# Loading block 0's x in quarters of 256 rows by half the columns, interleaved with the w1 chunks

## The chip, the cores and the metric

The kernel runs on one core of a Trainium2 chip. The metric is the device time of one execution in microseconds (us); where several executions were timed, their median is given. Times inside the kernel come from a hardware profile and are counted from the first instruction of its span.

## The reference

The reference is a feed-forward layer with a squared ReLU, in bfloat16:

```python
B, S, D, F = 1, 2048, 576, 4608
h = jnp.einsum("bsd,df->bsf", x, w1) + b1
r = jnp.where(h > zero, h, zero)
h = r * r
out = jnp.einsum("bsf,fd->bsd", h, w2) + b2
```

There are 2048 rows of x, 576 columns each (four groups of 128 and a remainder of 64), and 4608 hidden columns, which are 36 groups of 128.

## The kernel before

The 2048 rows are handled in four blocks of 512. The first product gives hT, the hidden values with the hidden columns on the partitions, so it needs x transposed. Blocks 1 to 3 get it by transposing transfers. Block 0 is loaded as it lies and transposed on TensorE, because that is sooner to start with. For the first six groups of hidden columns (the tile `qn`, "quads" of 128 rows of w1 by 768 columns), block 0 accumulates over full 128-row contractions in six PSUM banks `bk0`. All later groups use contractions of 64 rows, two at a time in the two halves of the array.

The loads that the opening needs, and where they are issued:

```python
def load_x(eng, j):                 # one tile of 128 rows by 576 columns, 144 KB
    eng.dma_start(out=xs[:, j, :], in_=x_view[:, j, :])

def load_quad(eng, c):              # 128 rows of w1 by 768 columns, 192 KB
    eng.dma_start(out=qn[:, c, :], in_=w1[c * P:(c + 1) * P, 0:G * P])

for j in range(RT):                 # RT = 4
    load_x(nc.sync, j)
    load_quad(nc.scalar, j)
nc.scalar.activation(out=warm[:], ..., func=ACT.Relu)
for h in range(2):
    load_rest(nc.sync, h)           # the last 64 rows of w1 for the same hidden columns
for j0, n in ((3, 1), (4, 1), ..., (14, 4)):
    for h in range(2):
        load_w1(nc.sync, h, j0, n, slice(0, NH))   # w1h, for the groups after these
```

A function that runs when the program is finished moves these first loads ahead of the barrier with which the program opens. Before, the first load of each of the two queues went ahead of the queue's drain instruction, the others ahead of its wait on the barrier:

```python
for k, i in enumerate(mine[:n]):
    wanted = mybir.InstDrain if k == 0 else mybir.InstEventSemaphore
```

While the loads are on their way, TensorE runs five matmuls of 128x512 on a constant, to bring up its clock. Then come the transposes (with the identity, built on GpSimd), the copies of their results from PSUM to `xT[0]`, and the matmuls on them:

```python
def transpose_tile(j, c, n, eng):   # n column groups of row tile j; eng copies them out of PSUM
    tp = psum.tile([P, n, P], BF16, name="tp", tag="bank")
    for k in range(n):
        d0 = (c + k) * P if c < NC else D - P
        nc.tensor.transpose(tp[:, k, :], xs[:, j, d0:d0 + P], ident[:])    # L178
    c0 = c if c < NC else 7
    copy_psum(eng, xT[0][:, c0:c0 + n, cols], tp[:])                        # L169 ScalarE, L171 VectorE
    if c == NC:
        copy_psum(eng, xT[0][0:H, 8, cols], tp[H:P, 0, :])

def full_mm(j, n, c):               # row tiles j to j+n-1, column group c of x
    cols = slice(j * P, (j + n) * P)
    for q in range(G):              # G = 6
        nc.tensor.matmul(bk0[q][:, cols], lhsT=qn[:, c, q * P:(q + 1) * P], rhs=xT[0][:, c, cols],
                         start=(j == 0 and c == 0), stop=False, ...)        # L228
```

After these the bias is transposed (L254), the last 64 rows are added (L259), the six banks go through ScalarE (ReLU with bias, L192) and VectorE (square, L194), and the steps on the remaining groups follow:

```python
for i in range(GP):
    for h in range(2):
        nc.tensor.matmul(bk0[GP * h + i][:], lhsT=qr[rows, i * P:(i + 1) * P],
                         rhs=xT[0][rows, place(h, 8), :], start=False, stop=True, ...)   # L259
...
for j in range(GP, NJ):
    a_step(0, j)                    # 18 matmuls of 64x512 each, L208
```

Blocks 1 to 3 run the same steps (L208). Then the second product follows: 64 of its columns at L321, the rest at L335.

Of the kernel before, what the change touches and what calls it, by code (L numbers as in the profile page):

```python
# [11 lines left out]
BF16 = mybir.dt.bfloat16  # L12
# [5 lines left out]
def kernel(  # L18
# [9 lines left out]
    nc = tc.nc  # L28
    P = 128
    H = 64  # L30
    x2 = x.flatten_outer_dims()
    out2 = out.flatten_outer_dims()
    S, D = x2.shape
    F = w1.shape[1]
    FH = F // 2
    G = 6
# [3 lines left out]
    NC = D // P  # L40
# [4 lines left out]
    RT = SB // P  # L45
    HALF = SB // 2
# [9 lines left out]
    psum = ctx.enter_context(tc.tile_pool(name="psum", bufs=8, space=PSUM))  # L56

    def bank(name):
        return psum.tile([P, SB], FP32, name=name, tag="bank")
# [10 lines left out]
    def early(n):  # L70
        at[0] += n
        assert at[0] <= NFT * D
        return w2_sb[:, at[0] - n:at[0]]


    xT = [early(XW).rearrange("p (w s) -> p w s", s=SB) for b in range(NSB - 1)]
    xT3 = xpool.tile([P, NH, SB], BF16, name="xT3", tag="xT3")
    xT.append(xT3[:])
    xs = early(RT * D).rearrange("p (j c) -> p j c", c=D)
# [6 lines left out]
    x_view = x2.rearrange("(rt p) d -> p rt d", p=P)  # L86
# [2 lines left out]
    def w2(ft, a, b):  # L89
        return w2_sb[:, ft * D + a:ft * D + b]  # L90

    def load_x(eng, j):
        eng.dma_start(out=xs[:, j, :], in_=x_view[:, j, :])

    def load_quad(eng, c):
        eng.dma_start(out=qn[:, c, :], in_=w1[c * P:(c + 1) * P, 0:G * P])  # L96

    def load_w1(eng, h, j0, n, cs):
        f0 = pairs[j0][h] * P
        eng.dma_start(out=w1h[h * H:(h + 1) * H, cs, j0 * P:(j0 + n) * P], in_=w1_rows[:, cs, f0:f0 + n * P])  # L100
# [5 lines left out]

    b1T = const.tile([P, NFT], FP32, name="b1T")
    warm = const.tile([P, 1], FP32, name="warm")
    for j in range(RT):
        load_x(nc.sync, j)  # L110
        load_quad(nc.scalar, j)
    nc.scalar.activation(out=warm[:], in_=nc.const_aps.tensor(1.0, [P, 1], FP32), func=ACT.Relu)
    for h in range(2):
        load_rest(nc.sync, h)
# [2 lines left out]
    for j0, n in ((3, 1), (4, 1), (5, 1), (6, 1), (7, 1), (8, 1), (9, 1), (10, 2), (12, 2), (14, 4)):  # L117
        for h in range(2):
            load_w1(nc.sync, h, j0, n, slice(0, NH))


    def issue_at_barrier(nc):
        entry, body = nc.main_func.blocks[:2]
        for engine in (mybir.EngineType.SP, mybir.EngineType.Activation):
            mine = [i for i in body.instructions if i.engine == engine and not isinstance(i, mybir.InstNoOp)]
            n = 0
            while isinstance(mine[n], mybir.InstDMACopy) and not mine[n].has_wait():
                n += 1
            assert n >= RT
            for k, i in enumerate(mine[:n]):  # L130
                wanted = mybir.InstDrain if k == 0 else mybir.InstEventSemaphore
                at = next(k for k, i in enumerate(entry.instructions) if i.engine == engine and isinstance(i, wanted))
                body.instructions.remove(i)
                entry.instructions.insert(at, i)

    nc.at_finalize(issue_at_barrier)


# [17 lines left out]
    ident = const.tile([P, P], BF16, name="ident")  # L156
# [10 lines left out]
    def copy_psum(eng, dst, src):  # L167
        if eng is nc.scalar:
            nc.scalar.copy(out=dst, in_=src)  # L169
        else:  # L170
            nc.vector.tensor_copy(out=dst, in_=src)  # L171

    def transpose_tile(j, c, n, eng):
        cols = slice(j * P, (j + 1) * P)
        tp = psum.tile([P, n, P], BF16, name="tp", tag="bank")
        for k in range(n):
            d0 = (c + k) * P if c < NC else D - P
            nc.tensor.transpose(tp[:, k, :], xs[:, j, d0:d0 + P], ident[:])  # L178
        c0 = c if c < NC else 7
        copy_psum(eng, xT[0][:, c0:c0 + n, cols], tp[:])  # L180
        if c == NC:
            copy_psum(eng, xT[0][0:H, 8, cols], tp[H:P, 0, :])

    def hT_of(b, ft):
        if b < NSB - 1:
# [30 lines left out]


    V, A = nc.vector, nc.scalar
    transpose_tile(0, 0, 1, V)
    transpose_tile(0, 3, 1, V)  # L220
    transpose_tile(0, 1, 2, A)
    transpose_tile(0, NC, 1, V)
    bk0 = [bank("ph") for _ in range(G)]

    def full_mm(j, n, c):
        cols = slice(j * P, (j + n) * P)
        for q in range(G):
            nc.tensor.matmul(bk0[q][:, cols], lhsT=qn[:, c, q * P:(q + 1) * P], rhs=xT[0][:, c, cols],  # L228
                             start=(j == 0 and c == 0), stop=False, skip_group_check=True)

    full_mm(0, 1, 0)
    transpose_tile(1, 0, 2, V)
    transpose_tile(1, 2, 2, A)
    full_mm(0, 1, 1)
    full_mm(1, 1, 0)
    transpose_tile(2, 0, 2, V)
    full_mm(1, 1, 1)
    transpose_tile(2, 2, 2, A)
    full_mm(0, 2, 2)
    transpose_tile(3, 0, 2, V)  # L240
    full_mm(2, 1, 0)
    full_mm(2, 1, 1)
    transpose_tile(3, 2, 2, A)
    full_mm(2, 1, 2)
    transpose_tile(1, NC, 1, V)
    full_mm(0, 2, 3)
    transpose_tile(2, NC, 1, V)
    full_mm(3, 1, 0)
    full_mm(3, 1, 1)
    transpose_tile(3, NC, 1, A)  # L250
    full_mm(3, 1, 2)
    full_mm(2, 2, 3)
    b1T_ps = psum.tile([P, P], BF16, name="b1T_ps", tag="bank")
    nc.tensor.transpose(b1T_ps[:], b1_rows[:], ident[:])  # L254
    nc.vector.tensor_copy(out=b1T[:], in_=b1T_ps[:, 0:NFT])
    for i in range(GP):
        for h in range(2):
            rows = slice(h * H, (h + 1) * H)
            nc.tensor.matmul(bk0[GP * h + i][:], lhsT=qr[rows, i * P:(i + 1) * P], rhs=xT[0][rows, place(h, 8), :],  # L259
                             start=False, stop=True, skip_group_check=True)  # L260
# [56 lines left out]
    for pr in range(NSB // 2):  # L317
        pc = bank("pc")
        for ft in range(NFT):
            for h in range(2):  # L320
                nc.tensor.matmul(pc[h * H:(h + 1) * H, :], lhsT=w2(ft, DM, D), rhs=hT_of(2 * pr + h, ft),  # L321
                                 start=(ft == 0), stop=(ft == NFT - 1))
# [52 lines left out]
```

## Time and profile before

| What | Value |
|---|---|
| Time, median of 3 runs | 290.41 us (289.91 to 290.61) |
| Span of the profiled execution | 288.3 us, granted TensorE clock 1.000 |
| TensorE (PE) busy | 284.7 us, 99% |
| ScalarE (ACT) busy | 95.4 us, 33% |
| VectorE (DVE) busy | 79.8 us, 28% |
| x loads, issue to landing, shortest / median / longest | 2.2 / 3.7 / 4.8 us |
| w1 quads, issue to landing, shortest / median / longest | 2.6 / 4.1 / 5.2 us |

PE is TensorE's matmul row and PEld its weight loads, which run beside the matmuls. A busy matmul row includes the time in which a matmul runs through the array, so the pace of a group is better read from the starts of one group and the next. "L228" is line 228 of the kernel before. The name `w_sb` stands for the whole of one large tile in which the loaded x, the quads and the transposed x of block 0 all lie until w2 takes it; a wait for `w_sb<-in_x_dram` is a wait for an x load, one for `w_sb<-in_w_dram` a wait for a w1 load. `ph` are the PSUM banks of the first product, `tp` those of the transposes.

### The profile page before, as it was taken

What the parts mean: (1) busy time and instruction counts of PE and PEld (TensorE: products, weight loads), DVE (VectorE), ACT (ScalarE), POOL (GpSimd) and SP (SyncE); (2) the same over time, 40 slices, a digit from 0 to 9 for tenths busy, and PEclk for the clock granted to TensorE, in tenths of its full rate; (3) what the DMA queues carried; (4) which work ended last, traced back from release to release, by engine and by line L of the source; (5) the groups of instructions that cost most, each with busy time, mean ns of one, the idle gap of its engine ahead of it and who ended that gap; (6) DMA issues with size and microseconds to landing.
All of it is one profiled execution on the core that took longest, in us unless ns stands there. A gap on an engine that the chain in (4) does not pass through costs nothing.

```text
span 288.3 us, 4894 instructions
## 1 busy us (share of the span) xinstructions
PE 284.7 (99%) x2108; PEld 134.4 (47%) x2108; DVE 79.8 (28%) x200; ACT 95.4 (33%) x154; POOL 1.5 (1%) x8
## 2 busy tenths in 40 slices
PE   8999999999999999999999999999999999999996
PEld 5644444444444444444445444444444444444454
DVE  2654444544444444444420011111100011111111
ACT  3676766666676666666620000000000000000000
POOL 2000000000000000000000000000000000000000
PEclk9999999999999999999999999999999999999999
DMA  8999999910400005300000100000000000000000
GB/s 240 190 207 201 180 178 208 314 61 0 125 0 2 1 2 150 98 0 2 0 3 18 20 20 20 23 20 8 12 23 20 20 20 23 20 20 22 23 20 20
DMA packets 35381, 18.31 MB, mean 64 GB/s; under 512 B 22804, under 2 KB 35360, under 8 KB 35360
## 3 DMA queue, kind: packets, MB, share of 16 engines
q1 hardware_dynamic: 34752, 17.21, 26.7%
q10 hardware_dynamic: 576, 0.79, 0.9%
q8 instruction: 16, 0.26, 0.4%
q14 instruction: 5, 0.04, 0.1%
q0 software_dynamic: 32, 0.01, 0.0%
HBM read 12.23 MB, written 2.36 MB: 51 GB/s over the span
## 4 chain that ended last, share of the span: by engine, by line
PE 97%; DMA 2%; ACTq 0%; issue 0%; DVE 0%
PE ph L208 46%; PE po L335 43%; PE pc L321 5%; DMA w_sb<-in_w_dram 2%; PE ph L228 1%; PE ph L259 0%; ACTq L96 0%; PE tp L178 0%; DVE o_sb L337 0%; ACTq L359 0%; PE b1T_ps L254 0%
## 5 line engine op out<-in xcount | busy, mean ns | idle before, releaser
L192 ACT ACTIVATE r<-ph,b1T 128x512 bf16<-128x512 f32 x144 | 90.6, 685 | 46.0 <-PE ph L208 45.1
L208 PE MATMUL ph<-w_sb,w1h 64*128 64x512 bf16 x918 | 99.2, 376 | 0.0
L208 PEld LDWEIGHTS <-w1h 64*128 64x128 bf16 x1242 | 60.4, 94 | 73.6
L335 PE MATMUL po<-w_sb,hT 128*128 128x512 bf16 x432 | 93.4, 379 | 0.0
L335 PEld LDWEIGHTS <-hT 128*128 128x128 bf16 x432 | 42.2, 98 | 51.2 <-issue 0.4
L194 DVE TENSOR_TENSOR hT<-r 128x512 bf16<-128x512 bf16 x108 | 45.7, 425 | 52.3 <-ACT r L192 52.2
L337 DVE TENSOR_TENSOR o_sb<-po,b_bc 128x512 bf16<-128x512 f32 (+2 forms) x17 | 11.2, 660 | 116.7 <-PE po L335 116.7
L208 PE MATMUL ph<-xT,w1h 64*128 64x512 bf16 x324 | 35.1, 376 | 0.0
L335 PE MATMUL po<-w_sb,w1h 128*128 128x512 bf16 (+2 forms) x180 | 31.3, 336 | 0.0
L335 PEld LDWEIGHTS <-w1h 128*128 128x128 bf16 x180 | 16.2, 98 | 15.3
L194 DVE TENSOR_TENSOR w1h<-r 128x512 bf16<-128x512 bf16 x36 | 15.3, 425 | 19.7 <-ACT r L192 19.5
L321 PE MATMUL pc<-hT,w_sb 128*64 128x512 bf16 x108 | 15.7, 379 | 0.0
L321 PEld LDWEIGHTS <-w_sb 128*64 128x64 bf16 x144 | 8.1, 110 | 7.6 <-issue 0.4
L321 PE MATMUL pc<-w1h,w_sb 128*64 128x512 bf16 x36 | 7.9, 379 | 0.0
L228 PE MATMUL ph<-w_sb 128*128 128x128 bf16 (+1 forms) x78 | 6.5, 232 | 0.0
L323 ACT ACTIVATE oc<-pc,b2T 128x512 bf16<-128x512 f32 x2 | 1.4, 687 | 13.7 <-PE pc L321 13.7
L228 PEld LDWEIGHTS <-w_sb 128*128 128x128 bf16 x78 | 5.3, 99 | 0.5 <-DMA w_sb<-in_w_dram 0.2
L331 DVE COPY o_sb<-oc 128x64 bf16<-128x64 bf16 x16 | 2.7, 172 | 9.2 <-DMA oc<-oc 9.2
L171 DVE COPY w_sb<-tp 128x128 bf16<-128x128 bf16 (+2 forms) x11 | 2.6, 243 | 6.4 <-PE tp L178 6.3
L169 ACT COPY w_sb<-tp 128x256 bf16<-128x256 bf16 (+2 forms) x6 | 2.0, 333 | 4.5 <-PE tp L178 4.5
L178 PE MATMUL tp<-ident,w_sb 128*128 128x128 bf16 x20 | 2.9, 243 | 0.4 <-DMA w_sb<-in_x_dram 0.4
L165 PE MATMUL wps<-one 128*128 128x512 bf16 x5 | 2.3, 626 | 0.4 <-DVE one L140 0.4
(26 smaller groups left out, 10.4 us busy)
## 6 DMA issues: line engine op xcount, KB each, us to landing
w_sb<-in_w_dram SPq DMA_DIRECT2D x2, 1728.0 KB, 8.4
out_dram<-o_sb SPq DMA_DIRECT2D x15, 144.0 KB, 1.8
w1h<-in_w_dram SPq DMA_DIRECT2D x14, 144.0 KB, 4.6
w_sb<-in_w_dram SPq DMA_DIRECT2D x2, 864.0 KB, 6.9
w1h<-in_w_dram SPq DMA_DIRECT2D x4, 288.0 KB, 6.4
w1h<-in_w_dram SPq DMA_DIRECT2D x2, 576.0 KB, 10.4
w1h<-in_w_dram SPq DMA_DIRECT2D x2, 432.0 KB, 6.7
w_sb<-in_w_dram ACTq DMA_DIRECT2D x4, 192.0 KB, 4.1
```

What stands on the lines that cost most here:

```text
L165: nc.tensor.matmul(wps[:], lhsT=ones[:, 0:P], rhs=ones[:], start=(i == 0), stop=(i == NWARM - 1))
L169: nc.scalar.copy(out=dst, in_=src)
L171: nc.vector.tensor_copy(out=dst, in_=src)
L178: nc.tensor.transpose(tp[:, k, :], xs[:, j, d0:d0 + P], ident[:])
L192: nc.scalar.activation(out=r[:], in_=bk[:], func=ACT.Relu, bias=b1T[:, ft:ft + 1], scale=1.0)
L194: nc.vector.tensor_tensor(out=hT_of(b, ft), in0=r3, in1=r3, op=ALU.mult)
L208: nc.tensor.matmul(bk[h][:], lhsT=w1h[rows, c, j * P:(j + 1) * P], rhs=xT[b][rows, place(h, c), :], start=(i == 0), stop=(i == NH - 1))
L228: nc.tensor.matmul(bk0[q][:, cols], lhsT=qn[:, c, q * P:(q + 1) * P], rhs=xT[0][:, c, cols], start=(j == 0 and c == 0), stop=False, skip_g ...
L321: nc.tensor.matmul(pc[h * H:(h + 1) * H, :], lhsT=w2(ft, DM, D), rhs=hT_of(2 * pr + h, ft), start=(ft == 0), stop=(ft == NFT - 1))
L331: nc.vector.tensor_copy(out=o_sb[:, DM:D], in_=o_tr[pr][:, jj, h * H:(h + 1) * H])
L335: nc.tensor.matmul(po[:, 0:e - a], lhsT=hT_of(b, ft)[:, jj, :], rhs=w2(ft, a, e), start=(ft == 0), stop=(ft == NFT - 1))
L337: nc.vector.tensor_tensor(out=o_sb[:, a:e], in0=po[:, 0:e - a], in1=b2_bc[:, a:e], op=ALU.add)
```

## The change

x of block 0 came in four row tiles of 128 rows by all 576 columns. It now comes in four quarters: the first or second 256 rows, by the first 256 or the last 320 columns. "xa01" are the left columns of row tiles 0 and 1, "xb23" the right ones of row tiles 2 and 3. The order of issue, over both queues, is xa01, q0, q1, xa23, xb01, q2, xb23, q3. The idea is that 256 rows of two column groups, with two chunks of w1, give TensorE more to do per byte than one row tile with all its columns. The transposes are regrouped accordingly: a chunk is one column group of 256 rows (two transposes into one bank, one copy), and all the full matmuls have 256 columns. Two loads of each queue, not one, now go ahead of the drain.

```diff
-    def load_x(eng, j):
-        eng.dma_start(out=xs[:, j, :], in_=x_view[:, j, :])
+    def load_x(eng, half, a, e):
+        js = slice(2 * half, 2 * half + 2)
+        eng.dma_start(out=xs[:, js, a:e], in_=x_view[:, js, a:e])
...
-    for j in range(RT):
-        load_x(nc.sync, j)
-        load_quad(nc.scalar, j)
+    CA = 2 * P
+    load_x(nc.sync, 0, 0, CA)
+    load_quad(nc.scalar, 0)
+    load_quad(nc.sync, 1)
+    load_x(nc.scalar, 1, 0, CA)
+    load_x(nc.sync, 0, CA, D)
+    load_quad(nc.scalar, 2)
+    load_x(nc.sync, 1, CA, D)
+    load_quad(nc.scalar, 3)
...
-                wanted = mybir.InstDrain if k == 0 else mybir.InstEventSemaphore
+                wanted = mybir.InstDrain if k < 2 else mybir.InstEventSemaphore
...
-    def transpose_tile(j, c, n, eng):
...
+    def transpose_chunk(half, c, eng):
+        cols = slice(half * HALF, (half + 1) * HALF)
+        d0 = c * P if c < NC else D - P
+        tp = psum.tile([P, HALF], BF16, name="tp", tag="bank")
+        for i in range(2):
+            nc.tensor.transpose(tp[:, i * P:(i + 1) * P], xs[:, 2 * half + i, d0:d0 + P], ident[:])
+        copy_psum(eng, xT[0][:, c if c < NC else 7, cols], tp[:])
         if c == NC:
-            copy_psum(eng, xT[0][0:H, 8, cols], tp[H:P, 0, :])
+            copy_psum(eng, xT[0][0:H, 8, cols], tp[H:P, :])
...
-    transpose_tile(0, 0, 1, V)
-    transpose_tile(0, 3, 1, V)
-    transpose_tile(0, 1, 2, A)
-    transpose_tile(0, NC, 1, V)
+    transpose_chunk(0, 0, V)
+    transpose_chunk(0, 1, V)
...
-    full_mm(0, 1, 0)
-    transpose_tile(1, 0, 2, V)
-    transpose_tile(1, 2, 2, A)
-    full_mm(0, 1, 1)
-    full_mm(1, 1, 0)
-    transpose_tile(2, 0, 2, V)
-    full_mm(1, 1, 1)
-    transpose_tile(2, 2, 2, A)
-    full_mm(0, 2, 2)
-    transpose_tile(3, 0, 2, V)
-    full_mm(2, 1, 0)
-    full_mm(2, 1, 1)
-    transpose_tile(3, 2, 2, A)
-    full_mm(2, 1, 2)
-    transpose_tile(1, NC, 1, V)
-    full_mm(0, 2, 3)
-    transpose_tile(2, NC, 1, V)
-    full_mm(3, 1, 0)
-    full_mm(3, 1, 1)
-    transpose_tile(3, NC, 1, A)
-    full_mm(3, 1, 2)
-    full_mm(2, 2, 3)
+    full_mm(0, 0)                      # full_mm(half, c, qs): 256 rows, column group c
+    full_mm(0, 1, range(2))
+    transpose_chunk(1, 0, V)
+    full_mm(0, 1, range(2, G))
+    transpose_chunk(1, 1, A)
+    full_mm(1, 0)
+    transpose_chunk(0, 2, V)
+    full_mm(1, 1)
+    transpose_chunk(0, 3, A)
+    full_mm(0, 2)
+    transpose_chunk(1, 2, V)
+    transpose_chunk(0, NC, A)
+    full_mm(0, 3)
+    transpose_chunk(1, 3, V)
+    full_mm(1, 2)
+    transpose_chunk(1, NC, A)
+    full_mm(1, 3)
```

The comment on the first new `full_mm` is added here; the rest of the diff only fits the helpers to the new arguments.

More of the change, by code (lines that the diff above doesn't have):

```diff
@@ L171, in copy_psum @@
             nc.vector.tensor_copy(out=dst, in_=src)
-    def transpose_tile(j, c, n, eng):
[L174 to L180, printed above, removed]
+    def transpose_chunk(half, c, eng):
[5 more added lines that the diff above has]
+        copy_psum(eng, xT[0][:, c if c < NC else 7, cols], tp[:])
         if c == NC:
-            copy_psum(eng, xT[0][0:H, 8, cols], tp[H:P, 0, :])
+            copy_psum(eng, xT[0][0:H, 8, cols], tp[H:P, :])
     def hT_of(b, ft):
@@ L218, with full_mm @@
     V, A = nc.vector, nc.scalar
-    transpose_tile(0, 0, 1, V)
-    transpose_tile(0, 3, 1, V)
-    transpose_tile(0, 1, 2, A)
-    transpose_tile(0, NC, 1, V)
+    transpose_chunk(0, 0, V)
+    transpose_chunk(0, 1, V)
     bk0 = [bank("ph") for _ in range(G)]
-    def full_mm(j, n, c):
-        cols = slice(j * P, (j + n) * P)
-        for q in range(G):
+    def full_mm(half, c, qs=range(G)):
+        cols = slice(half * HALF, (half + 1) * HALF)
+        for q in qs:
             nc.tensor.matmul(bk0[q][:, cols], lhsT=qn[:, c, q * P:(q + 1) * P], rhs=xT[0][:, c, cols],
-                             start=(j == 0 and c == 0), stop=False, skip_group_check=True)
-    full_mm(0, 1, 0)
-    transpose_tile(1, 0, 2, V)
-    transpose_tile(1, 2, 2, A)
-    full_mm(0, 1, 1)
-    full_mm(1, 1, 0)
-    transpose_tile(2, 0, 2, V)
-    full_mm(1, 1, 1)
-    transpose_tile(2, 2, 2, A)
-    full_mm(0, 2, 2)
-    transpose_tile(3, 0, 2, V)
-    full_mm(2, 1, 0)
-    full_mm(2, 1, 1)
-    transpose_tile(3, 2, 2, A)
-    full_mm(2, 1, 2)
-    transpose_tile(1, NC, 1, V)
-    full_mm(0, 2, 3)
-    transpose_tile(2, NC, 1, V)
-    full_mm(3, 1, 0)
-    full_mm(3, 1, 1)
-    transpose_tile(3, NC, 1, A)
-    full_mm(3, 1, 2)
-    full_mm(2, 2, 3)
+                             start=(half == 0 and c == 0), stop=False, skip_group_check=True)
+    full_mm(0, 0)
[15 more added lines that the diff above has]
+    full_mm(1, 3)
     b1T_ps = psum.tile([P, P], BF16, name="b1T_ps", tag="bank")
```

## The prediction

> **What bounds the kernel now.** I read the page's first part, then the chain that ended last, then who waited for whom in the opening microseconds, then the timeline of that stretch.
>
> ```profile
> PE 284.7 (99%) x2108; PEld 134.4 (47%) x2108; DVE 79.8 (28%) x200; ACT 95.4 (33%) x154; POOL 1.5 (1%) x8
> ```
>
> TensorE is busy for 99% of the span. The chain (start, length, what) says where the other 1% is:
>
> ```profile
> 1.13 4.82 DMA w_sb<-in_w_dram
> 5.95 0.05 issue
> 6.00 0.83 PE ph L228 x6
> ...
> 10.54 0.06 PE b1T_ps L254
> 10.59 0.76 PE ph L259 x6
> 11.35 134.03 PE ph L208 x1242
> 145.38 15.66 PE pc L321 x144
> 161.04 124.53 PE po L335 x612
> ```
>
> From 11.35 us on the chain is TensorE without a break: 134.03 + 15.66 + 124.53 us. The change touches none of it. Before 6.00 the chain is a transfer: the third w1 chunk, issued at 1.13 and landed at 5.95. So only the opening, up to the first L208 matmul, can move, and it moves the end one for one as long as the stream behind it stays unbroken. What it has to give is its idle time. The waits of PEld (the weight loads, which hold back their matmuls) in the first 30 us give it by cause, in total, times, longest:
>
> ```profile
> PEld L178 <- DMA w_sb<-in_x_dram: 1.2, 3, 0.6
> PEld L228 <- DMA w_sb<-in_w_dram: 0.2, 1, 0.2
> ```
>
> The timeline (start, length, engine, line; in brackets the idle time before) places them:
>
> ```profile
> 2.48 0.74 PE L178 MATMUL tp<-ident,w_sb 128*128 128x128 bf16 x5
> ...
> 3.11 0.51 PE L228 MATMUL ph<-w_sb 128*128 128x128 bf16 x6
> ...
> 4.04 0.23 PEld L178 LDWEIGHTS <-w_sb 128*128 128x128 bf16 x4 [0.60 <-DMA w_sb<-in_x_dram]
> ...
> 5.21 0.11 PEld L178 LDWEIGHTS <-w_sb 128*128 128x128 bf16 x2 [0.18 <-DMA w_sb<-in_x_dram]
> ...
> 5.99 0.55 PEld L228 LDWEIGHTS <-w_sb 128*128 128x128 bf16 x6 [0.22 <-DMA w_sb<-in_w_dram]
> 6.00 0.83 PE L228 MATMUL ph<-w_sb 128*128 128x256 bf16 x6
> 6.56 0.21 PEld L178 LDWEIGHTS <-w_sb 128*128 128x128 bf16 x2
> 6.66 0.28 PE L178 MATMUL tp<-ident,w_sb 128*128 128x128 bf16 x2
> 6.72 0.71 PEld L228 LDWEIGHTS <-w_sb 128*128 128x128 bf16 x12
> 6.78 0.83 PE L228 MATMUL ph<-w_sb 128*128 128x128 bf16 x12
> ```
>
> Here is what TensorE lacks: after six matmuls on the first x tile it has nothing until the second tile lands (4.0), then again at 5.2 and 6.0. After 6.0 the data is ahead of TensorE. The starts also give each form's true pace: six matmuls of 256 columns from 6.00 to 6.66, so 0.109 us each; two transposes from 6.66 to 6.78 and twelve matmuls of 128 columns from 6.78 to 7.45, so 0.056 us each.
>
> The stage from the first L228 (3.11) to the first L208 (11.18 by the timeline) lasts 8.07 us. Its work is 60 matmuls of 128 columns (3.36 us), 18 of 256 (1.96), 15 transposes (0.84), the bias transpose, 0.16 to the next start, and six L259 matmuls, from 10.53 to 11.18 (0.65): 6.97 us. So 1.1 us is idle. That is the whole prize, 0.4% of 290.41.
>
> **What the Trainium skill says.** "TensorE: Matmul & The Clock Gate", section "Back-to-back issue gap", gives columns / 2.4 + 2.5 ns once the clock is up, 56 and 109 ns for 128 and 256 columns; the trace has just that. The same page, "What's actually happening", says that the array runs at half rate until it has been busy for some 3.4 us, in a window that does not start with the kernel. Here the five warming matmuls take 0.43 us each (0.38 to 2.48, ending at the first transpose), the first five transposes 0.63 us together, and the full pace is there from 3.11, after 2.7 us. "DMA: Bandwidth & Descriptors", "Issuing engines are not separate DMA queues", says that transfers issued by SyncE and ScalarE share 16 engines and interleave. The trace agrees: all engines' mean DMA share is 1.02 from 2 to 4 us, with both queues loading. Its "Specifications" want 512 B or more in one piece for full rate; the w1 chunks behind, in pieces of 256 B, run at some 200 GB/s with the engines full (8 to 12 us), x and w1 quads at 309 (2 to 4 us). The new quarters have pieces of 512 and 640 B, on the right side of this.
>
> **The change, part by part.**
> *Bytes per unit of work.* Before, TensorE had after 336 KB (one x tile 144, one w1 quad 192) six matmuls of 128 columns, 0.34 us of work; after 672 KB another 18 of these. Now 128 + 192 KB give six matmuls of 256 columns (0.65 us), and 192 KB more, q1, another six. At 640 KB, with xa23, there are 24 such matmuls, 2.6 us, on the table. The load total stays 1344 KB; the order is better fitted to the arithmetic.
>
> *TensorE work removed.* 60 + 18 matmuls become 48 of 256 columns: 5.23 us in place of 5.32, so 0.09 saved. Twenty transposes stay twenty; now four of them come before the first L228 and sixteen after (0.90 in place of 0.84). Work from the first L228 on: 5.23 + 0.90 + 0.16 + 0.65 = 6.94 us.
>
> *First matmul.* The warming ends at 2.48, so x landing at 2.2 is not what holds the first transposes, and a slightly slower first quarter is hidden. In the timeline VectorE's first copy begins at 2.83, 0.35 after its single transpose. Now there are two, 0.11 apart at the slow clock, and the copy is 128x256, 0.29 us (the L171 group of that shape), not 0.23. That gives 2.48 + 0.11 + 0.35 + 0.29 = 3.23 and a hand-over of 0.05: 3.3. Before it was 3.11. So the start loses 0.2.
>
> *Transfers against need.* Running on from 3.3, six matmuls of step (0,0) end at 3.95, two of (0,1) at 4.17. Then xa23 is needed; two transposes, four matmuls, two transposes and (1,0) run to 5.5. Then xb01 is needed; after (1,1) at 6.3 q2 is needed, after (0,2) at 7.0 xb23, at 7.2 q3. For the arrivals I take the bytes by time from the windows of the trace: 254 KB moved by 2.0, 872 by 4.0, 1147 by 5.0. The last byte of the old set, at 1376 thousand bytes, was moved at about 5.7 and landed at 1.61 + 5.2 = 6.8 (last w1 issue and its longest landing), a lag of up to 1.1; the first pair lagged some 0.5. With 0.8 as the middle: xa23 (655 thousand bytes) moved at 3.3, there at 4.1; xb01 and q2 (1016) moved at 4.5, there at 5.3; all at 6.5 to 6.8. Against the needs 4.17, 5.5, 6.3, 7.0, 7.2 every one is just in time, the first two with hardly a margin. I count 0.15 us for waits left at xa23 and xb01 and for a late q0, which now shares the engines with q1, issued sooner.
>
> *Barrier.* Two transfers per queue now go ahead of each queue's drain. One issue takes about 0.4 us, so the barrier, released near 0.8 before, comes near 1.2 and the identity, ready at 1.49, near 1.9. The first transpose is at 2.48: hidden.
>
> *Copies.* VectorE and ScalarE have 292 and 367 ns copies of 256 columns with 0.6 us of matmuls between; only the last remainder is tight: transposed from 8.8, with ScalarE's copies from 9.03 for 0.37 + 0.26 us (the L169 groups), it is ready at 9.7, and L259 is due at 9.6. I count 0.1.
>
> *Sum.* 3.3 + 6.94 = 10.24 with no wait, against 11.18: 0.94 gained at best. Less 0.15 and 0.1 gives 0.7.
>
> **Behind the stage.** L208 starts some 0.7 earlier and wants its w1h chunks earlier. The chunks land 3.9 to 11.2 us after issue; by the semaphore times the tightest early one, column group 5, is there at 12.8 and used at 15.1. A start 1.0 earlier still leaves 1.3. ScalarE's six squared-ReLU evictions in a row shift with it, as each needs only L259 and the bias.
>
> **The rivals.** *The wait moves* (25%): q0 and q1 share the engines, q0 lands at 3.5, and xa23 comes at 4.5. For it: some packets take long, and landings spread by over 1 us in one transfer. It would eat 0.6 to 1.0: 289.9 to 290.4. *The transfer is hidden anyway* (5%): w1h or ScalarE give the gain back at 11 to 20 us; the idle time of TensorE there is now nil and the margin 2.3 us, so I doubt it: 290.3. *Slower* (7%): more and smaller pieces with strides take longer to issue and move, so that q3 ends after 7.8, or the full clock comes later: 290.4 to 290.9. *All the idle time goes* (15%), as when the full clock comes sooner: 289.4 or below.
>
> **Range and chances.** 290.41 − 0.7 = 289.7. The three runs of before lie within 0.7 us, so a median is good to some 0.3. With the gain between 0.1 and 1.2 in eight of ten cases, the range is 289.0 to 290.4. Two per cent is 5.8 us, over five times the idle time there is; the three chances follow.
>
> **What would show it.** The first L228 at 3.1 to 3.4; TensorE's idle time on DMA before 7 us at 0.3 in total, not 1.1; all L228 at 128x256, 48 of them; the first L208 near 10.5; L208, L321 and L335 of the same lengths as now. It is wrong if PEld waits 0.5 or more for q0 or xa23, if the identity or the remainder copies release a TensorE instruction, or if L208 shows a wait that it had not.

## The result, and the profile after

The changed kernel takes 291.81 us (median of 6 runs, 291.34 to 292.58), the kernel before, run beside it on the same chip, 290.02 us (289.71 to 290.61). The ratio is 1.0061, with a 95% interval of 1.0043 to 1.0080: the change makes the kernel slower by 1.8 us, where a gain of 0.7 was predicted.

The profiled execution of the changed kernel is the slowest of the six, 292.58 us against 290.04 for that of before, so the differences read below sum to 2.5 us, not to 1.8. In the changed file L186 is the transposes, L233 the 256-column matmuls, L215 the steps that were L208; L259, L321 and L335 are what they were.

The chain that ended last (start, length, what):

```profile
0.00 3.48 DMA w_sb<-in_x_dram
3.48 0.04 issue
3.52 0.41 PE tp L186 x2
3.94 0.02 issue
3.96 0.30 DVE w_sb L179
4.26 0.04 issue
4.30 1.86 PE ph L233 x8
...
8.94 0.77 PE ph L233 x6
9.71 0.11 PE tp L186 x2
9.82 0.66 PE ph L233 x6
...
12.65 0.38 ACT w_sb L177
13.03 0.04 issue
13.07 0.82 PE ph L259 x6
13.90 134.03 PE ph L215 x1242
147.93 15.66 PE pc L321 x144
163.59 124.53 PE po L335 x612
```

The three long pieces at the end are the same to the hundredth, 134.03, 15.66 and 124.53 us; they only start later. All of the loss is ahead of 13.90. Two things stand out there. The chain begins with the very first transfer, xa01, landed at 3.48 us; its counterpart x0 landed at 2.2. And the pace: six L233 matmuls take 0.66 us at 9.82, but eight take 1.86 at 4.30.

The waits of PEld in the first 30 us (in total, times, longest) show the same from the other side:

```profile
PEld L186 <- DMA w_sb<-in_x_dram: 1.7, 1, 1.7
...
PEld L259 <- DMA w1h<-in_w_dram: 0.2, 1, 0.2
```

There is one wait for a load, and it is for the first. The later waits, for x tiles and for the third w1 chunk, which the change was made to remove, are gone. The page names a w1h load for the last line; ScalarE's copies of the remainder are what ended at 13.03, as the chain's step before L259 says.

The timeline (start, length, engine, line; idle before in brackets) shows the hole between the warming and the first transposes:

```profile
0.38 2.31 PE L173 MATMUL wps<-one 128*128 128x512 bf16 x5 [0.38 <-DVE one L148]
...
1.69 0.29 POOL masks.py:199 TENSOR_SCALAR_AFFINE_SELECT ident<-ident 128x128 bf16<-128x128 bf16 x1
...
3.52 0.61 PE L186 MATMUL tp<-ident,w_sb 128*128 128x128 bf16 x4 [0.84 <-DMA w_sb<-in_x_dram]
...
4.30 1.86 PE L233 MATMUL ph<-w_sb 128*128 128x256 bf16 x8 [0.17 <-DVE w_sb L179]
...
13.72 2.55 PE L215 MATMUL ph<-w_sb,w1h 64*128 64x512 bf16 x22
```

The identity is ready at 1.98, so it holds nothing back. L233 starts at 4.30, not 3.11 (+1.19 us), and from there to the first L215 it is 9.42 us, not 8.07 (+1.35): together the 2.54 us. For the second part one asks for the duration of single L233 matmuls (shortest/median/longest in ns, then first and last start), once for the stretch from 4.3 to 8.9 us and once from 9.2 to 13:

```profile
L233 PE MATMUL ph<-w_sb x19: 372/417/417, 4.3 to 8.7; 128*128 128x256 bf16 x19
```

```profile
L233 PE MATMUL ph<-w_sb x29: 272/273/321, 9.0 to 12.6; 128*128 128x256 bf16 x29
```

A duration includes the run through the array; from start to start it is 0.213 us before and 0.109 after about 9.0. Until then TensorE ran at half rate. Nineteen matmuls of this form and six transposes at half pace cost 19 × 0.104 + 6 × 0.05 = 2.3 us more than at full pace. With the 6.94 us of work that the prediction counted and 0.2 us of wait at L259 this makes 9.4, and 9.42 were measured. The page's clock row shows 9 (90% or more) throughout and gives no sign of the half pace.

### The profile page after: what moved, and what is told of

Same layout as the page of the kernel before. It is cut to its first block, busy times and chain, and to the rows that moved or that the text cites. A ratio compares the mean times of both kernels' runs of the same rounds, so it can differ in the third digit from the quotient of the medians.

```text
span 290.8 us, 4830 instructions
## 1 busy us (share of the span) xinstructions
PE 286.6 (99%) x2078; PEld 144.4 (50%) x2078; DVE 78.9 (27%) x195; ACT 95.8 (33%) x154; POOL 1.5 (1%) x8
## 4 chain that ended last, share of the span: by engine, by line
PE 97%; DMA 1%; ACT 0%; DVE 0%; issue 0%
PE ph L215 46%; PE po L335 43%; PE pc L321 5%; PE ph L233 2%; DMA w_sb<-in_x_dram 1%; PE tp L186 1%; PE ph L259 0%; ACT w_sb L177 0%; DVE w_sb L179 0%; DVE o_sb L337 0%
## 5 line engine op out<-in xcount | busy, mean ns | idle before, releaser
L215 PEld LDWEIGHTS <-w1h 64*128 64x128 bf16 x1242 | 69.8, 94 | 64.3
L215 PE MATMUL ph<-w_sb,w1h 64*128 64x512 bf16 x918 | 99.2, 376 | 0.0
L335 PE MATMUL po<-w_sb,hT 128*128 128x512 bf16 x432 | 93.4, 379 | 0.0
L335 PEld LDWEIGHTS <-hT 128*128 128x128 bf16 x432 | 42.2, 98 | 51.1 <-issue 0.4
L215 PE MATMUL ph<-xT,w1h 64*128 64x512 bf16 x324 | 35.1, 376 | 0.0
L335 PE MATMUL po<-w_sb,w1h 128*128 128x512 bf16 (+2 forms) x180 | 31.3, 336 | 0.0
L335 PEld LDWEIGHTS <-w1h 128*128 128x128 bf16 x180 | 16.2, 98 | 15.3
L321 PE MATMUL pc<-hT,w_sb 128*64 128x512 bf16 x108 | 15.7, 379 | 0.0
L321 PEld LDWEIGHTS <-w_sb 128*64 128x64 bf16 x144 | 8.1, 110 | 7.6 <-issue 0.4
L233 PE MATMUL ph<-w_sb 128*128 128x256 bf16 x48 | 8.5, 330 | 0.2 <-DVE w_sb L179 0.2
L321 PE MATMUL pc<-w1h,w_sb 128*64 128x512 bf16 x36 | 7.9, 379 | 0.0
L233 PEld LDWEIGHTS <-w_sb 128*128 128x128 bf16 x48 | 5.4, 118 | 1.4 <-issue 0.3
L177 ACT COPY w_sb<-tp 128x256 bf16<-128x256 bf16 (+1 forms) x6 | 2.2, 371 | 7.1 <-PE tp L186 7.0
L179 DVE COPY w_sb<-tp 128x256 bf16<-128x256 bf16 x6 | 1.7, 292 | 9.8 <-PE tp L186 9.8
L186 PE MATMUL tp<-ident,w_sb 128*128 128x128 bf16 x20 | 3.1, 264 | 0.8 <-DMA w_sb<-in_x_dram 0.8
L186 PEld LDWEIGHTS <-w_sb 128*128 128x128 bf16 x20 | 2.1, 119 | 2.2 <-DMA w_sb<-in_x_dram 1.7
```

Of the source, the lines that this page charges most:

```text
L186: nc.tensor.transpose(tp[:, i * P:(i + 1) * P], xs[:, 2 * half + i, d0:d0 + P], ident[:])
L215: nc.tensor.matmul(bk[h][:], lhsT=w1h[rows, c, j * P:(j + 1) * P], rhs=xT[b][rows, place(h, c), :], start=(i == 0), stop=(i == NH - 1))
L335: nc.tensor.matmul(po[:, 0:e - a], lhsT=hT_of(b, ft)[:, jj, :], rhs=w2(ft, a, e), start=(ft == 0), stop=(ft == NFT - 1))
```

## The experiments

The question was which of three things made the first load late (its 256 pieces, the loads now issued sooner beside it, the bytes), and what made the clock late. All comparisons are with the kernel before, run on the same chip. A ratio is worked out from all the runs of both kernels and need not be the quotient of the two medians beside it.

### More warming

```diff
-    NWARM = 5
+    NWARM = 8
```

> The changed kernel with eight warming matmuls in place of five, so that TensorE has no hole between the warming (its end at 2.48 us) and the first quarter's landing (3.48). Theory (the hole kept the array at half rate until about 9 us): the pace of 0.109 us per 256-column matmul holds from the first or second L233 on; the first L233 stays near 4.2 because xa01 lands no sooner, and L215 starts near 11.5, so the time is 290.2 to 290.6. Rival (the moment of the full clock is chance and has nothing to do with the hole): L233 still runs at 0.213 until 7 to 9 us and the time stays at 291.3 to 292.5.

Measured: 290.57 us against 290.34, ratio 1.0007 (0.9996 to 1.0018). Filling the hole takes back nearly the whole loss, though the first L233 is 0.26 us later still. Even the slowest of the 20 runs, 291.23, is below the fastest of the changed kernel, 291.34, so chance alone does not explain the late clock, as the rival had it. The 20 runs fall in two groups, 12 at 290.1 to 290.6 and 8 at 291.1 to 291.2. The profiled one is of the latter (291.22):

```profile
0.38 3.59 PE L173 MATMUL wps<-one 128*128 128x512 bf16 x8 [0.38 <-DVE one L148]
3.76 0.63 PE L186 MATMUL tp<-ident,w_sb 128*128 128x128 bf16 x4
4.56 1.71 PE L233 MATMUL ph<-w_sb 128*128 128x256 bf16 x8 [0.17 <-DVE w_sb L179]
6.11 0.28 PE L186 MATMUL tp<-ident,w_sb 128*128 128x128 bf16 x2
6.22 0.60 PE L233 MATMUL ph<-w_sb 128*128 128x256 bf16 x4
```

Even here half pace lasts until about 6.0: transposes are 0.107 apart at 3.76, but four L233 are done in 0.43 from 6.22 to the next group at 6.65. So the hole is not all that decides. The theory holds for the time, and for the sign; "from the first or second L233 on" was too much.

### One load per queue ahead of the drain

```diff
-                wanted = mybir.InstDrain if k < 2 else mybir.InstEventSemaphore
+                wanted = mybir.InstDrain if k == 0 else mybir.InstEventSemaphore
```

> The changed kernel with one load per queue ahead of the drain, as before, so that q1 and xa23 are issued some 0.15 us later. Theory (xa01 is late because it comes in 256 pieces, and the pieces, not the bytes, are the limit in the first two microseconds): xa01 still lands after 3.0, the time stays within 0.5 of 291.8. Rival (q1 and xa23, issued sooner, take the transfer engines from xa01): xa01 lands by 2.4, the first L233 is near 3.3, and the time is 289.5 to 290.2.

Measured: 292.60 us (four runs) against 290.34, ratio 1.0082 (1.0065 to 1.0099). The first transposes:

```profile
3.21 0.61 PE L186 MATMUL tp<-ident,w_sb 128*128 128x128 bf16 x4 [0.52 <-DMA w_sb<-in_x_dram]
```

xa01 landed at 3.2, 0.3 sooner than in the changed kernel and still 1.0 later than x0. The same x0 load landed at 2.2 to 2.5 in the four profiles that have it, so 0.3 is no more than such a landing varies by. The loads beside it are at most a small part of the delay, and the time did not follow at all.

The converse, this part alone in the kernel before:

> The kernel before with two loads per queue ahead of the drain: this part of the change alone. Theory (harmless by itself): x0 lands by 2.3, the second tile some 0.1 to 0.2 earlier, the time within 0.3 of before. Rival (the early second loads hold up the first): x0 lands near 3, TensorE has a hole after its warming and the time is 291 or more.

Measured: 290.31 us against 290.34, ratio 0.9997 (0.9981 to 1.0013). It is harmless. x0 landed at 2.4.

### A shorter warming in the kernel before

```diff
-    NWARM = 5
+    NWARM = 3
```

> The kernel before with three warming matmuls in place of five: they end at 1.65 us, and until x0 lands at 2.2 TensorE has a hole of 0.5 us, and less activity in all ahead of it. Theory (a gap in the early activity delays the full clock): the opening runs at half pace for some microseconds more and the time is 0.7 to 2 us longer. Rival (the full clock comes at about 3.1 whatever TensorE does): no change, 289.8 to 290.3.

Measured: 291.72 us against 290.34, ratio 1.0044 (1.0024 to 1.0065), with runs from 290.22 to 293.0. Only the warming is cut, and it costs 1.3 us. Seven of its ten runs took more than 291.4 us, of the 37 of the kernel before only two. The profiled execution, 290.63, is one of the faster:

```profile
0.37 1.46 PE L165 MATMUL wps<-one 128*128 128x512 bf16 x3 [0.37 <-DVE one L140]
2.59 0.71 PE L178 MATMUL tp<-ident,w_sb 128*128 128x128 bf16 x5 [0.75 <-DMA w_sb<-in_x_dram]
3.19 0.80 PE L228 MATMUL ph<-w_sb 128*128 128x128 bf16 x6
3.99 0.58 PE L178 MATMUL tp<-ident,w_sb 128*128 128x128 bf16 x4
```

Six L228 of 128 columns, 0.34 us at full pace, run at 0.107 us each, at half pace, which here lasted until 5.8. A hole of 0.75 us and two matmuls fewer have done to the kernel before what xa01's lateness did to the changed one. This run changes the hole and the amount of warming together; it does not part them.

### Pieces or bytes

This is the disputed cost by itself, in the kernel before. Only x0's load is changed, to two overlapping pieces of 640 B per row; the transposes read the copy that has their columns:

```diff
-        eng.dma_start(out=xs[:, j, :], in_=x_view[:, j, :])
+        if j:
+            eng.dma_start(out=xs[:, j, :], in_=x_view[:, j, :])
+            return
+        src = bass.AP(tensor=x2.tensor, offset=0, ap=[[D, P], [D - PW, 2], [1, PW]])   # PW = 320
+        eng.dma_start(out=xs0.rearrange("p (k c) -> p k c", c=PW), in_=src)
```

> The kernel before, with only its first load changed: x0's 128 rows come as two overlapping pieces of 640 B each (columns 0 to 319 and 256 to 575) in place of one of 1152 B, so 256 pieces and 160 KB in place of 128 and 144; all else is as it was. Theory (the first load's landing is set by its number of pieces): x0 lands at 2.9 to 3.4 in place of 2.2, TensorE has a hole after its warming, and the time is 0.5 to 2 us longer. Rival (the bytes set it): x0 lands at 2.2 to 2.4, time 290.0 to 290.6.

Its control moves the same 160 KB in 128 pieces (the edit is against the run before it; the comment in that one is added here):

```diff
-        src = bass.AP(tensor=x2.tensor, offset=0, ap=[[D, P], [D - PW, 2], [1, PW]])
-        eng.dma_start(out=xs0.rearrange("p (k c) -> p k c", c=PW), in_=src)
+        src = bass.AP(tensor=x2.tensor, offset=0, ap=[[D, P], [1, 2 * PW]])
+        eng.dma_start(out=xs0, in_=src)
```

> The control to the run with x0 in two pieces per row: the kernel before, with x0's 128 rows as one piece of 1280 B each (the row and the first 64 columns of the next), so the same 160 KB in 128 pieces. Theory (the pieces set the landing): x0 lands by 2.5, time 290.0 to 290.7. Rival (the extra bytes did it): x0 lands near 3.3 and the time is 291.2 or more, as with two pieces.

Measured: in two pieces per row 291.53 us (four runs) against 290.46, ratio 1.0042 (1.0029 to 1.0056); in one long piece 290.61 against 290.62, ratio 1.0003 (0.9988 to 1.0018). The load's issue to landing, the one with two pieces per row first:

```profile
DMA to landing us min/median/max: 3.3/3.3/3.3
```

```profile
DMA to landing us min/median/max: 2.5/2.5/2.5
```

Same bytes, same place, same neighbours: twice the pieces is 0.8 us later, and 1.1 us in the kernel's time. The windows view shows where (stretch, length, five engines' busy time, clock, DMA share, GB/s), for the first two microseconds of the kernel before, the changed one, two pieces and the long piece:

```profile
0.00:2.00 2.00, 1.62 (x4) 0.57 (x5) 0.06 (x1) 0.00 (x0) 0.91 (x8) 1.00 0.43 127
```

```profile
0.00:2.00 2.00, 1.62 (x4) 0.58 (x5) 0.06 (x1) 0.00 (x0) 0.72 (x7) 1.00 0.28 69
```

```profile
0.00:2.00 2.00, 1.63 (x4) 0.58 (x5) 0.06 (x1) 0.00 (x0) 0.91 (x8) 1.00 0.35 71
```

```profile
0.00:2.00 2.00, 1.63 (x4) 0.59 (x5) 0.06 (x1) 0.00 (x0) 0.91 (x8) 1.00 0.45 105
```

With 256 pieces at the head 70 GB/s are moved, with 128 pieces 105 to 127, and the DMA share is lower too, so the engines were not full of short pieces: they had less to do. From 2 to 4 us the changed kernel moves 310 GB/s, as much as the kernel before.

The packets of SyncE's queue in the first 2.2 us (number, MB, share of the 16 engines' time), two pieces first, say the same:

```profile
q1 hardware_dynamic: 156, 0.10, 19.5%
```

```profile
q1 hardware_dynamic: 145, 0.17, 35.4%
```

About as many pieces, and little more than half the bytes. By the packets' times in all the traces, the 128th piece of x on this queue starts between 1.7 and 2.1 us with pieces of 512 to 1280 B, at 2.4 and 2.5 in the two runs with 2304 B. Where the first load has 256 pieces, its last starts at 2.6 to 2.9. So up to 1280 B pieces start at much the same pace whatever their length, and twice as many take longer.

### Both remedies, and other orders

The changed kernel with both edits above, eight warming matmuls and one load ahead of the drain:

> The changed kernel with eight warming matmuls and one load per queue ahead of the drain. Theory: xa01 at 3.2 to 3.5, the first L233 near 4.2, the full clock by about 6 at the latest, time 290.0 to 291.2 as with eight warming matmuls alone. Rival (the order of issue matters once the hole is gone): 289.7 or less.

Measured: 290.88 us against 290.46, ratio 1.0006 (0.9994 to 1.0019). As the theory had it. In the profiled execution (290.36 us) full pace came by 3.7 and nothing waited for a load after that:

```profile
3.67 0.39 PE L186 MATMUL tp<-ident,w_sb 128*128 128x128 bf16 x4
4.33 1.03 PE L233 MATMUL ph<-w_sb 128*128 128x256 bf16 x8 [0.27 <-DVE w_sb L179]
...
11.45 0.83 PE L215 MATMUL ph<-w_sb,w1h 64*128 64x512 bf16 x6
```

The first L215 was at 11.45, against 11.18 in the profile of before. With the clock in order the change is worth nothing: what it saves in waits it loses by the later start. Eleven of the 20 runs lie at 290.9 to 291.4, so the clock was probably not early in each of them.

The left columns by row tile, 128 pieces each, the w1 chunks on ScalarE (the loads are shown, with a comment added; the transposes and the first twelve matmuls go by row tile accordingly):

```diff
-    load_x(nc.sync, 0, 0, CA)
-    load_quad(nc.scalar, 0)
-    load_quad(nc.sync, 1)
-    load_x(nc.scalar, 1, 0, CA)
+    load_left(nc.sync, 0)              # xs[:, 0, 0:256]
+    load_quad(nc.scalar, 0)
+    load_left(nc.sync, 1)
+    load_quad(nc.scalar, 1)
+    load_x(nc.sync, 1, 0, CA)
     load_x(nc.sync, 0, CA, D)
     load_quad(nc.scalar, 2)
-    load_x(nc.sync, 1, CA, D)
     load_quad(nc.scalar, 3)
+    load_x(nc.sync, 1, CA, D)
```

> The changed kernel with the first quarter in two loads of 128 rows by 256 columns (128 pieces of 512 B each) on SyncE, the w1 chunks on ScalarE, and column group 0 of the first half in matmuls of 128 columns. Theory (what counts is how many pieces stand ahead of the first transposes): the first load lands by 2.2, TensorE has hardly a hole, the first L233-like matmul is at 3.2 to 3.6, and the time is 289.4 to 290.2. Rival (any left-columns-first order is late because the pieces of all loads together limit the start): the second load lands after 3.3, the time is 290.5 to 292.

> The same with six warming matmuls, ending at 2.9. If a hole of 0.2 to 0.4 us before the second load costs the clock, this is 0.3 us or more faster than with five; if there is none, the same or 0.1 slower.

Measured: 291.73 us against 290.46, ratio 1.0045 (1.0031 to 1.0058), and with six warming matmuls 291.32, ratio 1.0032 (1.0019 to 1.0045). The start was as hoped: first loads at 2.1 and 2.8, the first matmul at 3.28, full pace from 3.5. These are the 256 pieces of xa01, 512 B each, as two loads: 128 such short pieces landed as early as the 128 long ones of x0, so it is their number in a load that made xa01 late, not their length. But xa23, now behind these two on the same queue, landed at 6.2:

```profile
3.28 0.93 PE L250 MATMUL ph<-w_sb 128*128 128x128 bf16 x12
4.05 0.38 PE L244 MATMUL ph<-w_sb 128*128 128x256 bf16 x2
6.28 0.28 PE L191 MATMUL tp<-ident,w_sb 128*128 128x128 bf16 x2 [1.85 <-DMA w_sb<-in_x_dram]
```

The wait of 1.85 us took the place of the hole. Neither expectation had this: the theory's early start came true, its time did not. The version with six is faster by some 0.4 us, but the two intervals overlap. The hole that its expectation asked about is no answer either: in the profiles it was the version with six that ran at half pace up to its wait for xa23, which came 0.2 sooner, at 6.0.

### Fewer and longer pieces

Each partition takes two neighbouring rows of x, so 256 rows are 128 pieces of 2304 B. Block 0's output rows are written accordingly, the transposes and matmuls go in an order that suits whole rows, and one load goes ahead of the drain. The new loads, without the old calls that they replace:

```diff
-    def load_x(eng, half, a, e):
-        js = slice(2 * half, 2 * half + 2)
-        eng.dma_start(out=xs[:, js, a:e], in_=x_view[:, js, a:e])
+    x_rows2 = x2[0:SB, :].rearrange("(h p j) d -> h p (j d)", h=2, p=P)
+    def load_x(eng, half):
+        eng.dma_start(out=xs[:, 2 * half:2 * half + 2, :].rearrange("p j d -> p (j d)"), in_=x_rows2[half])
...
+    load_x(nc.sync, 0)
+    for c in range(3):
+        load_quad(nc.sync, c)
+    load_x(nc.sync, 1)
+    load_quad(nc.sync, 3)
```

> The opposite of the change: fewer and longer pieces. Each partition takes two neighbouring rows of x, so 256 rows come as 128 pieces of 2304 B; the halves of block 0 are whole rows, loaded on SyncE alone in the order x01, q0, q1, q2, x23, q3, and the output rows of block 0 are written back to their places. Theory: x01 (288 KB) lands by 2.7, the first 256-column matmul is at 3.3 to 3.6, and with hardly a wait after it the time is 289.3 to 290.1. Rival (288 KB before the first matmul are too many, whatever the pieces): x01 lands after 3.1, time 290.5 to 292.

> The same with q0, q2 and q3 issued by ScalarE, so that q0 shares the engines with x01. If the sharing matters, x01 lands 0.3 to 0.7 later than with one queue and the time is 0.3 to 1.5 longer; if not, the same within 0.2.

Measured: 291.39 us against 290.62, ratio 1.0037 (1.0024 to 1.0049); with q0, q2 and q3 on ScalarE 291.66, ratio 1.0038 (1.0022 to 1.0055). x01, 288 KB, landed at 2.9 from one queue and at 3.0 from two: more than twice the bytes of xa01, and half a microsecond sooner. But 2.9 is later than both x0 and the end of the warming, and x23 came at 6.9, when TensorE waited for it:

```profile
2.93 0.61 PE L184 MATMUL tp<-ident,w_sb 128*128 128x128 bf16 x4 [0.24 <-DMA w_sb<-in_x_dram]
...
6.96 0.28 PE L184 MATMUL tp<-ident,w_sb 128*128 128x128 bf16 x2 [0.27 <-DMA w_sb<-in_x_dram]
```

Half pace lasted until about 5.0 here. Neither the theory's landing (by 2.7) nor the rival's (after 3.1) came true: with as many pieces as x0, 144 KB more cost 0.4 to 0.8 us, so bytes count too. The time is in the rival's range. The sharing made no difference that counts.

Last, six warming matmuls in the kernel before:

> The kernel before with six warming matmuls, which end at about 2.9 us. Theory (the wait for x1 until 4.0 hides the first matmuls' delay of 0.4 us, and a fuller early stretch makes an early full clock likelier): the same to 0.4 us faster, and none of the runs above 291. Rival (the delay counts in full): 0.3 to 0.4 us slower.

Measured: 290.36 us against 290.51, ratio 0.9997 (0.9986 to 1.0007), with single runs up to 291.13. The 0.4 us of later start is hidden in the wait for x1; nothing is gained. No version here beats the kernel before.

## Why the prediction was wrong

**What bounds the kernel: right.** The long stream is unchanged to the hundredth, and the opening moved the end one for one: 2.54 us in the profiles' first L215, 2.54 in their times.

**The first matmul: the step that failed.** The prediction put "a slightly slower first quarter is hidden", and built 3.3 on the end of the warming. It worked out no landing for xa01 and took x0's 2.2 for its measure. xa01 landed at 3.48, 1.3 later than x0, and the sum of the same steps from the first transpose at 3.52 gives 4.3, as measured. For the later loads, too, it counted bytes alone, with a lag read from loads of 128 pieces. The two runs with 160 KB show that it is the pieces that make the delay: 2.5 us for 128, 3.3 for 256. That pieces of 512 and 640 B lie "on the right side" may hold for the GB/s of a stream under way; it does not carry over to the first load.

**The clock: left out.** The prediction quoted the Trainium skill ("TensorE: Matmul & The Clock Gate", "What's actually happening") on the half rate until the array has been busy for a while, and still took 0.109 us per matmul from the first one on. With a hole of 0.84 us after the warming, half pace lasted until 9.0, and the work of the stage took 2.3 us more than its 6.94. It weighed "the full clock comes later" only as part of a rival of 7%. Filling the hole brought the ratio from 1.0061 to 1.0007, so this, and not the late start by itself, is nearly all of the measured loss.

**Why the late start alone costs so little.** In the kernel before 1.1 us of waiting follow its early start. The changed kernel waits first and never again, as it was meant to. With the clock in order the first L215 comes at 11.45 instead of 11.18: the predicted 0.94 us of gain from 3.3, less one microsecond of later start, less 0.2 us of wait at the remainder.

**Transfers against need: right in the result, by luck.** From 4.30 on no matmul waited for x or a quad. But only xa23, at 4.2, landed as worked out: xb01 and q2 landed at 6.3 and 6.6 in place of 5.3, xb23 and q3 at 8.0 and 7.7 in place of 6.5 to 6.8. Half pace had moved the needs later by more than that: xb01 was transposed at 8.5, not 5.5. In the execution with full pace from 3.7 xb01 landed at 6.0 and was needed at 6.5; with the predicted start, a microsecond sooner, it would have been some 0.5 us late (an estimate from these times).

**Barrier: right**, the identity was ready at 1.98, against 1.9 predicted. **Remainder copies: right, though the wait was larger**, 0.2 us at L259 where 0.1 was counted. **Behind the stage: right**, no new wait in L215.

**The rivals.** The likeliest had the wait move to q0 and xa23; nothing waited for these. The nearest was "slower" (7%), which named both causes, smaller pieces and a later full clock. But it looked for the pieces at q3, the last load, not at the first, and allowed 0.5 us over the time before where 1.8 were lost.

What stays open is what limits the pace at which pieces start. The DMA share of 0.28 to 0.35 says that the engines were short of work in the first two microseconds, and that fits a limit on making or handing out pieces; no run here changed that pace. What sets the exact moment of the full clock is open too. In the kernel before 2.7 us of activity were enough; with eight warming matmuls, in the slower group, 5.6 us with hardly a gap were not.

## What to carry to other kernels

Count the pieces of the very first load, not only its bytes: at the start of a program 128 pieces of 1280 B were there 0.8 us before 256 of 640 B. A load that TensorE waited for right after its warming matmuls cost twice here when it was late, once by the wait and again by half pace for microseconds; so let the warming last until the load is there. When an order of loads is changed, work out the first arrival from a load with the same number of pieces.

## What the hardware showed that was not expected

The moment of full pace differs widely between executions. In the six profiles with a hole of 0.24 to 0.84 us between the warming and the first transposes it came between 5.0 and 9.0 us, in the eight without one between 3.1 and 6.1. So a hole delays it, but its absence does not make it early: in the control with the long piece, x0 was there when the warming ended, and half pace still lasted past 5.5, at 0.107 us for each of these twelve:

```profile
4.37 1.48 PE L238 MATMUL ph<-w_sb 128*128 128x128 bf16 x12
```

A single profile therefore says little about the moment; the spread of the timed runs says more.

A load of 256 pieces third in its queue (xa23 behind two left quarters) landed 5.1 us after its issue, while the same load second in the other queue took 3.7, with as many bytes issued ahead of it. Why was not tested.
